# Block products in the third chunk's feed-forward layer, with block weights and raw weights in buffers of their own

## The chip, the cores and the metric

One core of a Trainium2 chip runs the whole program. TensorE (PE) multiplies, VectorE (DVE) and ScalarE (ACT) work on elements, GpSimd (POOL) mostly issues DMAs here, and SyncE (SP) issues DMAs alone. The metric is the device time of one execution in microseconds (us). A profiled execution adds a span (first to last instruction) and the busy times of the engines.

## The reference

Two layers, each an attention block and a feed-forward block with residual additions, on x of 2048 rows and 576 columns, float32:

```python
def _A_ref(x, wqkv, wo):            # 32 heads of 18, window of 8 keys, dilation 2
    q, k, v = split(x @ wqkv)
    kg, vg = k[:, :, idx], v[:, :, idx]          # idx = pos - 2 * (0..7), masked below 0
    attn = softmax(einsum("bhsd,bhswd->bhsw", q, kg) * 18 ** -0.5)
    return einsum("bhsw,bhswd->bhsd", attn, vg) @ wo
def _B_ref(x, w1, w2):              # w1 576 x 4608, w2 4608 x 576
    return silu(x @ w1) @ w2
x = x + _A_ref(_layernorm(x), wqkv, wo)
x = x + _B_ref(_layernorm(x), w1, w2)
x = x + _A_ref(_layernorm(x), wqkv, wo)          # second layer, same weights
x = x + _B_ref(_layernorm(x), w1, w2)
```

## The kernel before

The rows are cut into four chunks of 512, and each chunk goes through both layers, so there are eight steps s = 0 to 7 (steps 0 to 3 are the first layer). A step is attention, the projection with wo (line 828), layer norm, and the feed-forward block. Keys, queries and values of chunks 1 to 3 in the first layer are computed during step 0 (`qkv_ahead`) and read back from HBM later.

All matrix products run in float16 halves: a value is split into a high half and a low half, and high by high, high by low and low by high are summed. The weights come as float32. ACT makes the high halves with a scale that is worked out from the squares of the weights, DVE makes the low halves, and the halves are stored to HBM (`w1s`, `w2s`, `wqs`) for the later steps. For w1 and w2 this happens in step 0, in `raw_load` and `raw_split`.

There are two forms of the feed-forward block. Steps 0 to 2 use `ffn`: for each of 36 slices of 128 hidden columns, 14 matmuls of 512 columns (line 1167), silu, splitting, and then the second product (line 1186, 72 matmuls of 288 columns for three slices and one block of rows). Steps 3 to 7 use `ffn_pairs`: two slices are taken together, and the first product of the pair is put together from seven block products of sums and differences (line 1071, seven matmuls of 256 columns each, 49 for a pair), in the manner of Strassen. `forms` makes the seven sums of the normalized input for a chunk, and DVE and ACT add up the products (lines 1075 and 1078) before silu. The second product is the same in size (line 1125). The 18 pairs go in groups of 5, 4, 5 and 4 (`G2`); 7 block weights and 2 slices of w2 are loaded for each.

The block weights are made once, by `prepare`, for each of the 18 pairs: POOL issues 12 DMAs that load a pair's w1 (lines 966 and 969), DVE makes three more sums (977), ACT makes the high halves (985), DVE the low halves (992), and POOL stores the seven block weights as `wfs` (997). They are loaded again by SP (`w<-wfs`).

What order the work has is settled at build time by a planner (`Plan.order`): each operation has an engine, an assumed duration and a priority (lower goes first), and the planner hands out buffers and writes each engine's instructions in one order. On the chip each engine follows its order and waits where data or a buffer is missing. `S2 = 3` is the first step that uses pairs, and `PREP = 1.6` is the priority of the prepares: behind the attention of step 2 (1.0) and ahead of that of step 3 (2.0). Areas of memory are shared by several kinds of buffers: `xa` (a normalized input, the prepares' output `wg`, half of the forms `yb`), `wq` (weights of q, k and v; the prepares' input `wr`, `ws`; two of the three buffers `hq` in which a pair's products are added), `w1` (six slices of w1 or twelve block weights), `w2`, `hs`, `xb`, `yo`, `o`.

At the very start `raw_wq` loads wqkv in four units of columns; each unit's five tiles are squared on ACT (line 565) before its scale is known, and then split (582 on ACT, 585 on DVE).

## Time and profile before

| What | Value |
|---|---|
| median of 3 runs | 2184.23 us (2181.3 to 2188.39) |
| profiled execution | 2180.11 us, span 2178.3 us |
| PE busy | 2125.9 us (98%) |
| DVE busy | 1585.8 us (73%) |
| ACT busy | 932.0 us (43%) |
| granted TensorE clock | 0.998 |
| HBM read, written | 298.47 MB, 67.68 MB |

The steps' feed-forward blocks follow each other on PE: in the trace that of step 0 begins at 226.9 us, of step 1 at about 473.6, of step 2 at 698.95, of step 3 (the first with pairs) at 932.2, and of step 7 at 1971.8. The attention of the next step is worked on by DVE while PE does a feed-forward block, and its matmuls stand in between. A busy share of an engine is an average over such stretches. The time the engine idles ahead of an instruction is listed with what ended that wait.

### The profile page before, as it was taken

What the parts mean: (1) busy time and instruction counts of PE and PEld (TensorE: products, weight loads), DVE (VectorE), ACT (ScalarE), POOL (GpSimd) and SP (SyncE); (2) the same over time, 40 slices, a digit from 0 to 9 for tenths busy, and PEclk for the clock granted to TensorE, in tenths of its full rate; (3) what the DMA queues carried; (4) which work ended last, traced back from release to release, by engine and by line L of the source; (5) the groups of instructions that cost most, each with busy time, mean ns of one, the idle gap of its engine ahead of it and who ended that gap; (6) DMA issues with size and microseconds to landing.
All of it is one profiled execution on the core that took longest, in us unless ns stands there. A gap on an engine that the chain in (4) does not pass through costs nothing.

```text
span 2178.3 us, 40221 instructions
## 1 busy us (share of the span) xinstructions
PE 2125.9 (98%) x15820; PEld 1540.8 (71%) x15820; DVE 1585.8 (73%) x2479; ACT 932.0 (43%) x1715; POOL 379.4 (17%) x639
## 2 busy tenths in 40 slices
PE   5999999999999999999999999999999999999999
PEld 3555556656766666677788778887688867888887
DVE  7898999999999754457975599646995569852222
ACT  7545677744244334343324434243442424333232
POOL 2124365332234331301100010000000000000000
PEclk9999999999999999999999999999999999999999
DMA  5577577586677675786649675496655855575443
GB/s 160 161 199 271 177 237 237 182 297 218 170 256 255 171 214 167 209 261 192 191 108 246 169 209 174 112 260 158 202 170 141 240 160 149 161 185 174 142 149 108
DMA packets 314006, 416.07 MB, mean 191 GB/s; under 512 B 136904, under 2 KB 237876, under 8 KB 307544
## 3 DMA queue, kind: packets, MB, share of 16 engines
q1 hardware_dynamic: 274832, 279.13, 45.2%
q0 software_dynamic: 35712, 129.17, 18.3%
q10 hardware_dynamic: 3272, 5.19, 0.8%
q8 instruction: 124, 2.03, 0.4%
q14 instruction: 66, 0.54, 0.1%
HBM read 298.47 MB, written 67.68 MB: 168 GB/s over the span
## 4 chain that ended last, share of the span: by engine, by line
PE 71%; DVE 15%; DMA 7%; issue 3%; POOL 1%; ACT 1%; ACTq 0%; SPq 0%; DVEq 0%; POOLq 0%
PE acc L1125 23%; PE z L1071 10%; PE misc L1071 10%; PE acc L1186 7%; PE z L1167 6%; PE z L658 6%; PE misc L658 5%; PE acc L828 4%; DVE pr L789 2%; DVE lg L760 2%; DMA w<-wfs 2%; DVE pr L796 2%; DVE pr L756 2%; DMA wq<-in_B_w_dram 1%; DVE xa L992 1%
## 5 line engine op out<-in xcount | busy, mean ns | idle before, releaser
L1125 PE MATMUL acc<-w,h 128*128 128x288 f16 x4320 | 544.9, 286 | 1.5 <-DVE h L1104 0.7
L1125 PEld LDWEIGHTS <-h 128*128 128x128 f16 x4320 | 422.5, 98 | 108.6 <-DVE h L1104 1.0
L1071 PEld LDWEIGHTS <-w 128*128 128x128 f16 x4410 | 430.8, 98 | 64.4 <-DMA w<-wfs 7.4
L1167 PE MATMUL z<-xb,w 128*128 128x512 f16 x1512 | 331.8, 379 | 6.4 <-ACT w L902 2.0
L1186 PE MATMUL acc<-w,h 128*128 128x288 f16 x2592 | 321.9, 286 | 0.0
L1186 PEld LDWEIGHTS <-h 128*128 128x128 f16 x2592 | 253.7, 98 | 65.7
L1071 PE MATMUL z<-xb,w 128*128 128x256 f16 x2240 | 281.9, 273 | 2.5 <-DMA w<-wfs 1.3
L1071 PE MATMUL misc<-xb,w 128*128 128x256 f16 x2170 | 273.4, 273 | 5.5 <-DMA w<-wfs 4.5
L1167 PEld LDWEIGHTS <-w 128*128 128x128 f16 x1512 | 147.5, 98 | 182.3 <-DVE w L904 3.7
L835 DVE SCALAR_TENSOR_TENSOR x<-acc,d,x 128x576 f32<-128x576 f32 x135 | 109.5, 812 | 192.3 <-PE acc L1125 151.5
L658 PEld LDWEIGHTS <-xa 128*128 128x128 f16 x1344 | 132.3, 99 | 119.6 <-issue 10.1
L756 DVE TENSOR_TENSOR pr<-qt,kv 128x2304 f32<-128x2304 f32 x64 | 163.5, 2554 | 33.6 <-DMA kv<-kv 32.2
L789 DVE TENSOR_TENSOR pr<-kv,pe 128x1152 f32<-128x1152 f32 x128 | 169.7, 1352 | 1.1
L760 DVE TENSOR_REDUCE lg<-pr 128x128 f32<-128x2304 f32 x64 | 163.1, 2548 | 1.2
L796 DVE TENSOR_TENSOR pr<-pr 128x1152 f32<-128x1152 f32 (+1 forms) x128 | 135.2, 1056 | 3.4
L1169 ACT ACTIVATE hs<-z,d 128x512 f32<-128x512 f32 x108 | 73.8, 683 | 123.1 <-PE z L1167 121.4
L1104 DVE SCALAR_TENSOR_TENSOR h<-wq,sh,h 128x1024 f16<-128x1024 f32 x59 | 75.5, 1280 | 60.9 <-ACT h L1101 60.9
L658 PE MATMUL z<-wq,xa 128*128 128x432 f16 x602 | 116.3, 349 | 3.4 <-ACT w L671 3.1
L828 PE MATMUL acc<-wo,yo 128*128 128x288 f16 x896 | 115.7, 288 | 3.3 <-DMA yo<-yh 3.3
L658 PE MATMUL misc<-wq,xa 128*128 128x432 f16 x574 | 111.8, 351 | 4.0 <-ACT xa L448 2.5
L1174 DVE SCALAR_TENSOR_TENSOR h<-hs,sh,h 128x512 f16<-128x512 f32 x108 | 79.6, 746 | 45.6 <-ACT h L1171 45.5
L1075 ACT ACTIVATE wq<-misc 128x256 f32<-128x256 f32 x85 | 32.0, 376 | 187.0 <-PE misc L1071 187.0
(196 smaller groups left out, 2355.1 us busy)
## 6 DMA issues: line engine op xcount, KB each, us to landing
w<-wfs SPq DMA_DIRECT2D x630, 160.0 KB, 3.3
w<-w2s SPq DMA_DIRECT2D x252, 288.0 KB, 4.8
w<-w1s SPq DMA_DIRECT2D x72, 320.0 KB, 4.8
wfs<-xa POOLq DMA_DIRECT2D x18, 1120.0 KB, 5.7
wq<-wqs SPq DMA_DIRECT2D x17, 1080.0 KB, 7.0
kv<-kd POOLq DMA_DIRECT2D x8, 1584.0 KB, 8.2
w1s<-w POOLq DMA_DIRECT2D x36, 320.0 KB, 3.8
w<-in_B_w_dram POOLq DMA_DIRECT2D x36, 288.0 KB, 4.6
```

Source lines behind the costliest of these rows:

```text
L658: nc.tensor.matmul(T(m)[:, :3 * UC], a, b, start=n == 0, stop=n == len(pl) - 1)
L756: nc.vector.tensor_tensor(T(pr), T(qt)[:, j:j + 2, None, :].to_broadcast([P, 2, W, UC]), win(T(kv), j, 2), op=ALU.mult)
L760: nc.vector.tensor_reduce(T(lg)[:, j:j + 2].rearrange("p a w h -> p (a w h)"), T(pr).rearrange("p a w (h d) -> p (a w h) d", d=DH), axis=A ...
L789: nc.vector.tensor_tensor(T(pr)[:, a].rearrange("p w (h d) -> p w h d", d=DH), v, T(pe)[:, j + a, :, :, None].to_broadcast([P, W, UH, DH]) ...
L796: nc.vector.tensor_tensor(t[:, :, 0:h, :], t[:, :, 0:h, :], t[:, :, h:2 * h, :], op=ALU.add)
L828: nc.tensor.matmul(T(acc)[:, h, 0:288], a, b[:, h * 288:(h + 1) * 288], start=n == 0, stop=n == len(pl) - 1)
L835: nc.vector.scalar_tensor_tensor(t, T(acc)[:, :, 0:288], d, t, op0=ALU.mult, op1=ALU.add)
L1071: nc.tensor.matmul(t, w[:, u, :], v[:, r, :], start=first and m == 0, stop=m == 6, skip_group_check=True)
L1125: nc.tensor.matmul(T(acc)[:, h, 0:288], T(hb[t])[:, a, f, j * P:(j + 1) * P], T(wbs[t][f])[:, w, h * 288:(h + 1) * 288], start=t == 0 and ...
L1167: nc.tensor.matmul(T(z), v, u, start=m == 0, stop=m == len(pl) - 1)
L1174: op("DVE", 0.68, lambda hs=hs, h=h, f=f: nc.vector.scalar_tensor_tensor(T(h)[:, 1, :], T(hs), shs[i][:, f:f + 1], T(h)[:, 0, :], op0=ALU. ...
L1186: nc.tensor.matmul(T(acc)[:, h, 0:288], T(hb[q])[:, a, j * P:(j + 1) * P], T(wbs[q][0])[:, w, h * 288:(h + 1) * 288], start=q == 0 and m = ...
```

## The change

Step 2 uses pairs as well (`S2 = 2`), so the prepares must be done for it. They get the priority 0.9, ahead of the attention of step 2. So that they can overlap with step 2's feed-forward block, buffers are placed anew. The block weights are stored in two parts from two buffers, `wg` with four rows and `wh` with three, and a pair's load waits only for its part. The forms of step 2 use `yc`, which lies in the second of the two key and value buffers, in place of `yb`. The products of a pair are added in `ha` (in the areas `hs`, `xb` and `yo`) up to step 6. The prepare's load is made of 8 DMAs instead of 12, for the same bytes; the last 32 rows of each half are read four times through a step of zero.

In step 0, from slice 6 on (`FAR = 6`), raw w2 goes to `wu` (in `xa`) and the halves of w1 to `wv` (in `wq`), where before both shared the buffers of `w1` and `w2`. And at the start, the squares of the second unit of wqkv wait until ACT has made the fourth high half of the first unit. Some assumed sizes for the planner are changed too, and fetches and sums of attention 3 wait for step 2's forms.

```diff
+FAR = 6
-PREP = 1.6
-S2 = 3
+PREP = 0.9
+S2 = 2
...
-    part("wg", XA, 1, [7, 5, P], F16)
+    part("wg", XA, 1, [4, 5, P], F16)
+    part("wh", XA, 1, [3, 5, P], F16, at=4 * KB * 2)
...
-    tag("kv", 2, [P, NI, 2, UC], F32)
+    KVB = NI * 2 * UC * 4
+    KV = area("kvs", 2 * KVB, F32)
+    part("kv", KV, 2, [NI, 2, UC], F32)
+    part("yc", KV, 1, [8, KH], F32, at=KVB, turns=False)
...
+    part("wv", WQA, 6, [10, P], F16)
+    part("wu", XA, 4, [2, D], F16)
...
+    parts("ha", [(HSA, 0), (XB, 14 * KB * 2), (YO, 0)], [4, 2 * P], F32)
...
-            op("ACT", 0.7 + (1.3 if u == 0 and k == 0 else 0), square, [rs[k]], [("accq", u, k)], WQ[u])
+            op("ACT", 0.7 + (1.3 if u == 0 and k == 0 else 0), square, [rs[k]], [("accq", u, k)], WQ[u], after=highs[3:4] if u else ())
...
-            op("ACT", 0.57, hi, [rs[k], ("su", u)], [w.keys[k]], WQ[u])
+            highs.append(op("ACT", 0.57, hi, [rs[k], ("su", u)], [w.keys[k]], WQ[u]))
...
-        a, b = raws[f] = Buf("w1"), Buf("w2")
+        far = f >= FAR
+        a, b = raws[f] = Buf("w1"), Buf("wu" if far else "w2")
...
-        wab = [(Buf("w1"), Buf("w2")) for f in fs]
+        far = f0 >= FAR
+        wab = [(Buf("wv" if far else "w1"), Buf("w2")) for f in fs]
...
-            for i in range(4):
-                f, h = divmod(i, 2)
-                c = slice((2 * q + f) * P, (2 * q + f + 1) * P)
-                nc.gpsimd.dma_start(t[:, i, 0:2, :], w1[h * KH:h * KH + 2 * P, c].rearrange("(k p) c -> p k c", p=P))
-            for r in range(4):
-                for h in range(2):
-                    nc.gpsimd.dma_start(t[32 * r:32 * (r + 1), h:4:2, 2, :], w1[
-                        h * KH + 2 * P:(h + 1) * KH, 2 * q * P:(2 * q + 2) * P].rearrange("p (f c) -> p f c", f=2))
-        op("POOL", 7.2, load, ["wsc"], [w], prio, nbytes=P * 12 * P * 4, lanes=8)
+            for h in range(2):
+                for k in range(2):
+                    nc.gpsimd.dma_start(t[:, h:4:2, k, :], w1[h * KH + k * P:h * KH + (k + 1) * P, 2 * q * P:(2 * q + 2) * P].rearrange(
+                        "p (f c) -> p f c", f=2))
+                for f in range(2):
+                    v = w1[h * KH + 2 * P:(h + 1) * KH, (2 * q + f) * P:(2 * q + f + 1) * P]
+                    nc.gpsimd.dma_start(t[:, h + 2 * f, 2, :], bass.AP(tensor=v.tensor, offset=v.offset, ap=[[0, 4], *v.ap]))
+        op("POOL", 4.8, load, ["wsc"], [w], prio, nbytes=P * 12 * P * 4, lanes=8)
...
-        op("POOL", 0.57, lambda: nc.gpsimd.dma_start(wfs[q], T(g).rearrange("p i a b -> p (i a b)")), [(g, 0), (g, 4)],
-           [("wfs", q)], prio, nbytes=P * 7 * KB * 2)
+            op("POOL", 0.57, lambda g=g, r0=r0, r1=r1: nc.gpsimd.dma_start(
+                wfs[q][:, r0 * KB:r1 * KB], T(g).rearrange("p i a b -> p (i a b)")), [(g, 0)], [("wfs", q, r0 // 4)], prio, nbytes=P * n * KB * 2)
...
-                hq, h = Buf("hq"), Buf("hp")
+                hq, h = Buf("hq" if s >= NC - 1 else "ha"), Buf("hp")
...
-        XT[s] = layer_norm(X[s], s - 1.0, "xb", s == 1, s == 0) if s < S2 else forms(X[s], s - 1.0)
+        XT[s] = layer_norm(X[s], s - 1.0, "xb", s == 1, s == 0) if s < S2 else forms(X[s], s - 1.0, "yc" if s == S2 else "yb", [("wfs", NP - 1, 1)] if s == S2 + 1 else [])
```

In the changed kernel the lines lie some 9 to 16 further down: 565 becomes 577, 582 becomes 594, 977 becomes 992, 992 becomes 1007, 997 becomes 1012, 1078 becomes 1094 and 1104 becomes 1120.

The first place is ACT at the start: `junk` with 128x432 are the squares of wqkv, `yo` and `yh` the first rows normalized, `wq` the high halves, `xa` the transposed input. Before:

```order
L565 ACT_TABLE_LOAD
L565 ACTIVATE junk,accq<-h 128x432 x9
L522 ACTIVATE yo<-x_74,nt_99 128x576
L525 ACTIVATE yh<-yo,nt_99 128x576
L582 ACTIVATE wq<-h,su 128x432 x4
L448 ACTIVATE xa<-acc_105 128x9x128
```

And in the changed kernel:

```order
L577 ACT_TABLE_LOAD
L577 ACTIVATE junk,accq<-h 128x432 x5
L534 ACTIVATE yo<-x_74,nt_98 128x576
L537 ACTIVATE yh<-yo,nt_98 128x576
L594 ACTIVATE wq<-h,su 128x432 x4
L457 ACTIVATE xa<-acc_104 128x9x128
L594 ACTIVATE wq<-h,su 128x432
```

Four squares of the second unit, which stood ahead of the first normalization, have moved behind the high halves.

The second place is POOL with the prepares, between the second and third steps' feed-forward blocks. `wq` is here the area that takes the raw weights. Before:

```order
L997 DMA wfs_207<-xa 128x4480
L966 DMA wq<-in_B_w_dram 128x2x128 x4
L969 DMA wq<-in_B_w_dram 32x2x128 x8
L997 DMA wfs_208<-xa 128x4480
L966 DMA wq<-in_B_w_dram 128x2x128 x4
```

And in the changed kernel:

```order
L1012 DMA wfs_209<-xa 128x2560
L1012 DMA wfs_209<-xa 128x1920
L713 DMA kvs<-kd_241 128x3168
L715 DMA qt_84<-qd_233 128x576
L1012 DMA wfs_210<-xa 128x2560
L1012 DMA wfs_210<-xa 128x1920
L981 DMA wq<-in_B_w_dram 128x2x128 x2
L985 DMA wq<-in_B_w_dram 128x1x128 x2
```

A store has become two, and a load of 12 issues one of 8 (two such pairs of rows).

The third place is DVE where step 2's feed-forward block begins. `pr`, `lg` and `pe` belong to attention 3, `x` to the second product, `h` to the low halves of the hidden values, `wq<-wq` and `xa` to a prepare. Before:

```order
L1174 SCALAR_TENSOR_TENSOR h<-hs,sh_267,h 128x512
L774 TENSOR_REDUCE mx_91<-pe_88 128x32
L775 RECIPROCAL mx_91<-mx_91 128x32
L776 TENSOR_TENSOR pe_88<-pe_88,mx_91 128x256
L789 TENSOR_TENSOR pr_89<-kv_83,pe_88 128x1152
L1174 SCALAR_TENSOR_TENSOR h<-hs,sh_267,h 128x512
L977 TENSOR_TENSOR wq<-wq 128x384 x4
```

And in the changed kernel:

```order
L1007 SCALAR_TENSOR_TENSOR xa<-wq,accw,xa 128x3x128
L848 SCALAR_TENSOR_TENSOR x_81<-acc_104,d_269,x_81 128x576
L1094 TENSOR_TENSOR hs<-z_100,hs 128x256
L1094 TENSOR_TENSOR hs<-misc_102,hs 128x256
L1094 TENSOR_TENSOR hs<-z_101,hs 128x256
L769 TENSOR_TENSOR pr_88<-qt_84,kvs 128x2304
L1094 TENSOR_TENSOR yo<-misc_102,yo 128x256
L1094 TENSOR_TENSOR yo<-misc_103,yo 128x256
L1120 SCALAR_TENSOR_TENSOR h<-hs,sh_267,h 128x1024
```

In the order of before, DVE reaches this place with the sums of prepare 9 of 18, in the last of attention 3's four units. In the changed order 13 of the 18 prepares stand ahead of the first addition for a pair, and the other five in between the pairs; attention 3 is here at its second unit.

## The prediction

> **What bounds the kernel.** I read the page first: the busy times, and then the chain that ended last by engine.

> ```profile
> span 2178.3 us, 40221 instructions
> PE 2125.9 (98%) x15820; PEld 1540.8 (71%) x15820; DVE 1585.8 (73%) x2479; ACT 932.0 (43%) x1715; POOL 379.4 (17%) x639
> PE 71%; DVE 15%; DMA 7%; issue 3%; POOL 1%; ACT 1%; ACTq 0%; SPq 0%; DVEq 0%; POOLq 0%
> ```

> PE idles 2178.3 - 2125.9 = 52.4 us in all. A busy PE may still be slow, so I cut the span at the steps' feed-forward blocks and read the busy times by stretch. Behind the comma stand the busy us of PE, PEld (weight loads), DVE, ACT and POOL, then the granted clock, the DMA share and GB/s; the two rows of the second fence are of PE alone.

> ```profile
> 226.90:473.60 246.70, 240.88 (x1590) 154.00 (x1590) 234.24 (x364) 167.36 (x287) 117.06 (x204) 1.00 0.68 225
> 473.60:698.95 225.35, 225.35 (x1469) 143.44 (x1467) 221.66 (x274) 88.29 (x117) 70.68 (x119) 1.00 0.71 226
> 698.95:932.20 233.25, 229.92 (x1482) 145.33 (x1480) 134.80 (x235) 88.17 (x139) 73.93 (x124) 0.99 0.69 199
> 932.20:1190.00 257.80, 256.30 (x2075) 202.38 (x2074) 188.61 (x293) 100.79 (x202) 20.70 (x33) 1.00 0.68 193
> 1190.00:1450.00 260.00, 256.65 (x2077) 202.92 (x2076) 186.44 (x291) 95.78 (x196) 16.40 (x28) 1.00 0.67 181
> 1450.00:1711.00 261.00, 257.80 (x2086) 203.62 (x2084) 184.96 (x286) 96.12 (x196) 10.65 (x20) 1.00 0.66 181
> 1711.00:1971.80 260.80, 259.26 (x2101) 205.24 (x2100) 182.61 (x280) 95.78 (x196) 10.66 (x20) 1.00 0.63 177
> 1971.80:2178.30 206.50, 202.28 (x1746) 170.59 (x1744) 57.12 (x90) 67.13 (x126) 0.54 (x1) 1.00 0.45 141
> ```

> ```profile
> 0.00:49.20 49.20, 25.65 (x165) 1.00 0.61 172
> 49.20:226.90 177.70, 171.75 (x1047) 0.99 0.64 198
> ```

> The reader sees three things. PE is the bound from 226.9 us to the end: it idles 5.8 us in step 0's block, 0 in step 1's, 3.3 in step 2's, and 1.5, 3.4, 3.2, 1.5 and 4.2 in the five blocks with pairs. Nearly half of all its idling, 23.6 us, lies in the first 49.2 us. And DVE is nearly as full in steps 0 and 1 (221.66 of 225.35 us in the second row), but has 98.5 us free in step 2's block, the one that is changed. So a change pays by the work that it takes off PE, and by idle time at the start, as long as DVE and the loads keep up.

> **Term 1, the first product of step 2.** What a matmul takes in a stream is read from long pieces of the chain, which are start, length and what:

> ```profile
> 771.43 27.20 PE z L1167 x126
> 798.62 26.46 PE acc L1186 x216
> 932.39 3.06 PE z L1071 x28
> 2000.01 27.93 PE acc L1125 x228
> ```

> A matmul of 512 columns takes 27.20 / 126 = 0.2159 us, one of 256 takes 3.06 / 28 = 0.1093. The second product costs 0.1225 us a matmul in both forms (26.46 / 216 and 27.93 / 228), and has 864 of them in either. Direct: 36 x 14 x 0.2159 = 108.8 us. Pairs: 18 x 49 x 0.1093 = 96.4 us. This takes 12.4 us off PE, and in step 2's block (third row) PE works 229.92 of 233.25 us, so it is all on the path: -12.4.

> [...]

> **Term 2, the squares at the start.** Here are, in this order, rows of ACT, of DVE and of PE from the timeline. In brackets stands the idle time ahead and what ended it.

> ```profile
> 12.80 0.19 ACT L565 ACTIVATION_READ_ACCUMULATOR junk<-h 128x1 f32 x1
> 15.79 0.56 ACT L565 ACTIVATE junk<-h 128x432 f16<-128x432 f32 x1 [2.80 <-DMA h<-in_A_wqkv_dram]
> 18.88 0.76 ACT L522 ACTIVATE yo<-x,nt 128x576 f32<-128x576 f32 x1
> 20.36 2.28 ACT L582 ACTIVATE wq<-h,su 128x432 f16<-128x432 f32 x4
> ```

> ```profile
> 13.97 0.16 DVE L476 TENSOR_SCALAR nt<-mv 128x4 f32<-128x4 f32 x1
> ```

> ```profile
> 20.50 0.61 PE L446 MATMUL acc<-ident,yh 128*128 128x128 f16 x4 [3.06 <-ACT yh L525]
> 24.71 5.22 PE L658 MATMUL misc<-wq,xa 128*128 128x432 f16 x14 [2.51 <-ACT xa L448]
> ```

> The first unit's squares end at 13.0, and the normalization's numbers `nt` are there at 14.1. Yet ACT next has four squares of the second unit in its order, whose load lands at 15.8, and so the normalization begins at 18.88. With the squares behind, it can begin at 14.15: 4.7 us earlier. PE's first real product follows later on. From the rows' lengths: the row block on ACT ends at 15.7, the four high halves at 18.0, and DVE needs until about 20.9 for the low halves of two row blocks and of the weights, which it makes one after the other. PE's transposes then end at 21.4, so the product at 24.71 moves to about 21.5. That is -3.2 us. The bounds are -4.7 (all of it) and 0 (the second unit's weights come too late by as much, since its own squares now come later). Of the stretch behind, 49.2 to 226.9, PE works 171.75 of 177.70 us, so an earlier start is passed on.

> **Term 3, waits of step 2's block.** Its 3.3 us of idle is a single row:

> ```profile
> 740.77 4.93 PE L828 MATMUL acc<-wo,yo 128*128 128x288 f16 x28 [3.33 <-DMA yo<-yh]
> ```

> The first row below is DVE's, the second is one of the chain.

> ```profile
> 727.84 0.51 DVE L815 TENSOR_SCALAR yh<-o,so 128x576 f16<-128x576 f32 x1
> 729.90 10.82 DMA yo<-yh
> ```

> The projection of chunk 3 (line 828) stands on PE at 740.77, and its first input was made by DVE only at 727.84. In the changed order PE meets it later, behind 686 matmuls of the pairs' first product and 552 of the second: 698.95 - 3.2 + 686 x 0.1093 + 552 x 0.1225 = 838 us. On DVE, the order's rows up to this input, each priced with the mean of its group, come to 91 us more than before: 727.84 + 91 - 3.2 = 816 us, if DVE never waits. So 22 us are left for the rest of the input's split and for the transposing DMA, which took 10.8 us there. The old wait of 3.3 may go wholly, or come again: I take half, -1.7, bounds -3.3 and +3.3.

> Pairs bring waits of their own. The five blocks with pairs idle 1.5 to 4.2 us, 2.8 on average, the one cause that stands out being late block weights:

> ```profile
> PE misc L1071 <- DMA w<-wfs: 4.5, 3, 2.4
> ```

> I take +2.8 for the new block of pairs; bounds +1.5 and +12 (second rival).

> **What is costed at nothing.** DVE gets 4 additions and a split of 1024 columns for a pair, and loses two splits of 512:

> ```profile
> L1174 DVE SCALAR_TENSOR_TENSOR h<-hs,sh,h 128x512 f16<-128x512 f32 x108 | 79.6, 746 | 45.6 <-ACT h L1171 45.5
> L1104 DVE SCALAR_TENSOR_TENSOR h<-wq,sh,h 128x1024 f16<-128x1024 f32 x59 | 75.5, 1280 | 60.9 <-ACT h L1101 60.9
> L1078 DVE TENSOR_TENSOR wq<-z,wq 128x256 f32<-128x256 f32 x92 | 37.7, 419 | 21.5 <-ACT wq L1075 12.8 <-PE z L1071 8.6
> ```

> That is 18 x (4 x 0.419 + 1.280 - 2 x 0.746) = 26.4 us. Steps 1 and 2 together have 221.66 + 134.80 = 356.5 us of DVE work in 458.6 us; with 26.4 more in 12.4 less it is 383 of 446, still covered. If the cover goes, PE waits in its second products, as rival 1 says. The prepares are only moved. Their 12 DMA issues become 8 and their one store becomes two, 10 for 13 on POOL, which works 70.68 and 73.93 us in the two stretches: no cost. Where the waits `after` are added (fetch and sums of attention 3 behind the forms), what queues behind them on POOL are prepares' loads; with 13 of 18 prepares ahead of the pairs I cost that at nothing too. Step 0's new buffers can change its 5.8 us of idle either way; PE has no other slack there, so I take 0, bounds -5.8 and +5.8.

> **The sum.** -12.4 - 3.2 - 1.7 + 2.8 = -14.5 us. The profiled execution took 2180.11 us (span 2178.3), 4.1 below the median of 2184.23. So it becomes 2165.6, and the median 2169.7. With all bounds at their best it is -12.4 - 4.7 - 3.3 + 1.5 - 5.8 = -24.7, or 2159.5.

> **Rival 1, slower: the prepares come too late.** A pair's products wait for its `wfs`. The stores in the profile before:

> ```profile
> L997 POOL DMA_DIRECT2D wfs<-xa x18: 537/569/804, 535.9 to 945.1; - x18
>   DVE xa L992: 101.9, 11
> DMA to landing us min/median/max: 5.1/5.7/8.6
> w<-wfs SPq DMA_DIRECT2D x630, 160.0 KB, 3.3
> ```

> 18 stores from 535.9 to 945.1 are one in 24.1 us. In the new order 43 us less DVE work stand ahead of the first sums (436 for 479 us, priced as above), so the first store comes at about 535.9 - 43 = 493. At the old pace the last is issued at 493 + 17 x 24.1 = 903, and is loaded 5.7 + 3.3 us later, at 912. PE needs it at 695.8 + 17 x 5.36 (first products) + 14 x 48 x 0.1225 (second products of three groups) + 112 x 0.1225 (a projection) = 883. It would wait 29 us, and the sum turns to +14: 2199 us. This decides once the pace is above 22.4 us a prepare. Against it speaks that the store's waits are for DVE (101.9 us of them), that is, for an order which put attention first; the new order puts 13 prepares ahead of the first pair. Chance 0.12.

> **Rival 2, no change: loads starve the pairs.** A pair's loads are 7 x 160 + 2 x 288 KB against 2 x (320 + 288) KB, 8.6 MB more for 18, which over 220 us is 39 GB/s on top of the 226 that step 1's block with prepares shows at a share of 0.71. If each of the four groups then waits some 3 us for a load (the longest such wait in the trace is 2.4), the waits are +12 in place of +2.8: -5.3, or 2178.9 us, within the bound of no change. Chance 0.10; at this bandwidth no row shows PE waiting, but none shows pairs.

> **Rival 3, no change: the narrow products gain nothing.** By busy time, not by the stream, the products of both forms cost a pair the same:

> ```profile
> L1167 PE MATMUL z<-xb,w 128*128 128x512 f16 x1512 | 331.8, 379 | 6.4 <-ACT w L902 2.0
> L1071 PE MATMUL z<-xb,w 128*128 128x256 f16 x2240 | 281.9, 273 | 2.5 <-DMA w<-wfs 1.3
> ```

> 331.8 / 1512 x 28 = 6.14 us and 281.9 / 2240 x 49 = 6.17 us. Then term 1 is 18 x 0.03 = +0.5, and the sum -1.6: 2182.6 us. But busy intervals of neighbours in different banks overlap and are counted in both lines, so the chain's 3.06 us for 28 is the better measure. Chance 0.03. [...]

> **Rival 4, no change: the start is not passed on.** The second unit's weights come later by what the first gains, and step 0's new order waits 5.8 us more: -14.5 + 3.2 + 5.8 = -5.5, 2178.7 us. DVE, which follows the same chain at the start, speaks against. Chance 0.07.

> **The numbers.** The forecast, 2169.7 us, has a chance of 0.68. A measurement of this kernel tells a change of about 0.3% (6.5 us, so below 2177.7 is faster and above 2190.8 slower). Faster is the forecast, 0.68; same are rivals 2, 3 and 4, 0.20; slower is rival 1, 0.12. The range goes from 2158, the sum of the best bounds with a little for the runs' spread, to 2185, which takes in rivals 2 to 4 and leaves out rival 1. The forecast's own range is 2160 to 2177.

> **What would show it.** Term 1: step 2's block has 882 matmuls of 256 columns, and PE's busy time falls by about 12 us. Term 2: ACT's first `yo` begins near 14 us and the first product of 14 near 21.5. Term 3: the row of PE's waits for `yo<-yh` shrinks, and that for `w<-wfs` stays below 9 us. Rival 1 would show as PE waiting for `w<-wfs` at the end of the third step, rival 2 as waits spread over all four groups. The prediction fails if PE idles more than 50 us in all, or if DVE, full until chunk 3's projection, comes to it later than PE does.

## The result: no change

The changed kernel takes 2185.23 us (median of 14 runs, 2177.21 to 2187.70), the kernel before 2184.54 us in the same session (14 runs, 2179.49 to 2190.68). The ratio is 1.000 with a 95% interval of 0.999 to 1.001. The forecast was 2169.7 us, so 15 us of expected gain are missing. The profiled execution took 2186.47 us with a span of 2184.3 us, against 2180.11 and 2178.3 before.

One thing in the words ahead of the prediction is wrong: the products of a pair are added in `ha` in step 2 alone, and not up to step 6. The line reads `Buf("hq" if s >= NC - 1 else "ha")` with four chunks, so steps 3 to 7 use `hq` as they did before. No term of the prediction rests on it.

### The profile page after: what moved, and what is told of

It is laid out like the page before. It is cut to its first block, busy times and chain, and to the rows that moved or that the text cites. A ratio compares the mean times of both kernels' runs of the same rounds, so it can differ in the third digit from the quotient of the medians.

```text
span 2184.3 us, 41276 instructions
## 1 busy us (share of the span) xinstructions
PE 2119.9 (97%) x16198; PEld 1578.8 (72%) x16198; DVE 1605.7 (74%) x2539; ACT 954.5 (44%) x1795; POOL 364.3 (17%) x585
## 4 chain that ended last, share of the span: by engine, by line
PE 81%; DVE 8%; DMA 7%; ACT 2%; issue 1%; POOL 1%; SPq 0%; ACTq 0%; DVEq 0%
PE acc L1141 25%; PE misc L1087 11%; PE z L1087 11%; PE z L670 8%; PE acc L1202 8%; PE z L1183 7%; PE misc L670 5%; PE acc L841 4%; DMA w<-wfs 3%; DVE lg L773 1%; DVE pr L802 1%; DVE pr L769 1%; DVE pr L809 1%; DMA w<-w2s 1%; DMA wq<-in_B_w_dram 1%
## 5 line engine op out<-in xcount | busy, mean ns | idle before, releaser
L1087 PEld LDWEIGHTS <-w 128*128 128x128 f16 x5292 | 518.9, 98 | 97.3 <-DMA w<-wfs 21.4
L1087 PE MATMUL z<-xb,w 128*128 128x256 f16 x2653 | 339.2, 275 | 14.0 <-DMA w<-wfs 9.9
L1087 PE MATMUL misc<-xb,w 128*128 128x256 f16 x2639 | 333.9, 273 | 10.4 <-DMA w<-wfs 8.6
L769 DVE TENSOR_TENSOR pr<-qt,kvs 128x2304 f32<-128x2304 f32 x64 | 163.4, 2553 | 34.6 <-DMA kvs<-kvs 24.7
L802 DVE TENSOR_TENSOR pr<-kvs,pe 128x1152 f32<-128x1152 f32 x128 | 169.9, 1352 | 1.1
L1183 PE MATMUL z<-xb,w 128*128 128x512 f16 x588 | 130.8, 383 | 6.0 <-ACT w L918 2.4
L841 PEld LDWEIGHTS <-yo 128*128 128x128 f16 x896 | 88.1, 99 | 27.1 <-DMA yo<-yh 2.7
L750 POOL DMA_DIRECT2D kvs<-kvs x64 | 33.8, 535 | 374.8 <-ACT qt L740 348.1
L1183 PE MATMUL z<-xb,wq 128*128 128x512 f16 x420 | 93.2, 379 | 0.7 <-ACT hs L1185 0.7
```

The lines of the kernel that those rows point to most:

```text
L769: nc.vector.tensor_tensor(T(pr), T(qt)[:, j:j + 2, None, :].to_broadcast([P, 2, W, UC]), win(T(kv), j, 2), op=ALU.mult)
L802: nc.vector.tensor_tensor(T(pr)[:, a].rearrange("p w (h d) -> p w h d", d=DH), v, T(pe)[:, j + a, :, :, None].to_broadcast([P, W, UH, DH]) ...
L841: nc.tensor.matmul(T(acc)[:, h, 0:288], a, b[:, h * 288:(h + 1) * 288], start=n == 0, stop=n == len(pl) - 1)
L1087: nc.tensor.matmul(t, w[:, u, :], v[:, r, :], start=first and m == 0, stop=m == 6, skip_group_check=True)
L1183: nc.tensor.matmul(T(z), v, u, start=m == 0, stop=m == len(pl) - 1)
```

## The profile after

The page's first lines and its chain by engine:

```profile
span 2184.3 us, 41276 instructions
PE 2119.9 (97%) x16198; PEld 1578.8 (72%) x16198; DVE 1605.7 (74%) x2539; ACT 954.5 (44%) x1795; POOL 364.3 (17%) x585
PE 81%; DVE 8%; DMA 7%; ACT 2%; issue 1%; POOL 1%; SPq 0%; ACTq 0%; DVEq 0%
```

PE's busy time fell by 6.0 us and its idle time rose from 52.4 to 64.4 us. Where that lies is read from the same cuts as before: the start, step 0's attention, the feed-forward blocks of steps 0, 1 and 2, and all the rest. The last fence has the rest of the kernel before. Columns as in the prediction: busy us of PE, PEld, DVE, ACT, POOL, then granted clock, DMA share and GB/s.

```profile
0.00:43.00 43.00, 23.99 (x165) 14.69 (x166) 33.70 (x122) 31.61 (x65) 11.55 (x24) 1.00 0.69 192
43.00:220.76 177.76, 171.50 (x1046) 98.28 (x1045) 162.08 (x250) 98.57 (x188) 47.27 (x67) 0.99 0.63 196
220.76:467.15 246.39, 241.14 (x1592) 154.51 (x1590) 231.65 (x366) 170.83 (x292) 121.99 (x210) 0.99 0.71 231
467.15:698.39 231.24, 227.51 (x1468) 143.72 (x1466) 205.32 (x297) 104.14 (x158) 83.78 (x124) 0.99 0.84 244
698.39:932.14 233.75, 219.66 (x1861) 182.39 (x1858) 175.32 (x269) 98.14 (x183) 41.22 (x60) 0.98 0.79 227
932.14:2184.30 1252.16, 1236.14 (x10076) 985.18 (x10073) 797.65 (x1239) 451.20 (x910) 58.49 (x101) 1.00 0.61 173
```

```profile
932.20:2178.30 1246.10, 1232.30 (x10076) 984.74 (x10074) 799.74 (x1240) 455.61 (x916) 58.95 (x102) 1.00 0.63 176
```

| Stretch | before | after | difference |
|---|---|---|---|
| until step 0's block begins | 226.9 | 220.76 | -6.1 |
| step 0's block | 246.7 | 246.4 | -0.3 |
| step 1's block | 225.35 | 231.24 | +5.9 |
| step 2's block (the one with new pairs) | 233.25 | 233.75 | +0.5 |
| steps 3 to 7 | 1246.1 | 1252.16 | +6.1 |

So the start gave its gain and step 1 gave it back. In step 2's block PE works 219.66 us for 229.92, as hoped, but it idles 14.1 us for 3.3. PE's rows there, from the timeline:

```profile
709.85 2.62 PE L1141 MATMUL acc<-w,h 128*128 128x288 f16 x20 [1.64 <-DVE h L1120]
720.89 1.68 PE L1087 MATMUL z<-xb,w 128*128 128x256 f16 x7 [8.42 <-DMA w<-wfs]
731.59 0.93 PE L1087 MATMUL z<-xb,w 128*128 128x256 f16 x7
732.36 0.93 PE L1087 MATMUL misc<-xb,w 128*128 128x256 f16 x7
```

One wait, 8.42 us for a block weight of the second pair, is 60% of the idle time. Behind it seven matmuls took 1.68 us, where a row of seven takes 0.93 further on: the granted clock was 0.53 from 720.90 to 727.00 us. What SP's queue did in that place (rows of the queue's own timeline, then of its waits between 680 and 760 us):

```profile
692.71 9.82 SPq L858 DMA_DIRECT2D w<-w2s x9
705.01 31.62 SPq L1017 DMA_DIRECT2D w<-wfs x24
```

```profile
SPq L1017 <- DMA w<-w2s: 12.6, 7, 2.8
SPq L858 <- PE acc L1202: 5.3, 8, 3.0
```

Nine loads of w2 (288 KB each) stand ahead of the second pair's last block weights. They wait for buffers that step 1's last products free, and the block weights behind them then wait 12.6 us more for w2 loads to land. The reason is in the trace: in this program SP's loads take turns on eight semaphores, and each waits until the eighth one ahead of it has landed. The block weight's load at 705.01 us waits so for the w2 load that was issued at 693.44. At 688 us, 5 us ahead of the w2 loads, POOL had issued two fetches of attention 3; the DMA view of 670 to 735 us has them as

```profile
kvs<-kd POOLq DMA_DIRECT2D x2, 1584.0 KB, 10.6
```

so either the order on SP's queue or the burst of bytes could be the cause. That was the first question for experiments. The second was why the start's gain did not arrive.

## The experiments

All were timed against the kernel before on the same chip; a ratio within 0.003 of 1 is no change by the prediction's bound.

**Block weights ahead of w2.** In the first group of step 2, the w2 loads of the first three pairs go behind these pairs' block weights (`wfl[2]` is the last load of those):

```diff
-                w2b = [load_w2(2 * q + f, pd) for f in range(2)]
+                if g or s > S2:
+                    w2b = [load_w2(2 * q + f, pd) for f in range(2)]
+                else:
+                    if q == 2:
+                        first = [load_w2(f, pd, after=[wfl[2]]) for f in range(6)]
...
```

> The changed kernel, but in the first group of step 2 the loads of w2 for the first three pairs stand on SP's queue behind the block weights of those pairs. Queue theory: the wait of 8.42 us for w<-wfs at 720.89 came from the nine w2 loads (2.6 MB) ahead of the block weights. It falls below 2 us, the halved clock of 10.24 us behind it goes as well, and the time falls by 8.4 + 5.1 = 13 us, to about 2172 (ratio 0.994). Rival, burst theory: the transfers were slow since the fetches of attention 3 (3.75 MB), two stores and a prepare's loads fell into the same 10 us; the block weights then still land late, a wait of 4 us or more stays in the first three pairs, and the time falls by less than 5 us.

It took 2173.35 us, ratio 0.9956 (0.9941 to 0.9971): faster than both kernels. Step 2's block (its row among the stretches) and SP's queue at its start:

```profile
698.65:920.58 221.93, 218.50 (x1868) 181.88 (x1865) 173.65 (x272) 98.27 (x184) 41.20 (x60) 1.00 0.82 241
```

```profile
699.60 10.89 SPq L1019 DMA_DIRECT2D w<-wfs x14
714.31 7.19 SPq L858 DMA_DIRECT2D w<-w2s x8
```

PE idles 3.4 us there in place of 14.1, the granted clock is 1.00 where it was 0.98, and the block is 11.8 us shorter. That is the whole difference of the medians (11.9, or 11.0 when each is set against its own runs of the kernel before). So with these bytes the queue's order decides. The expectation had counted 5.1 us for the halved clock; of that stretch of 10.24 us 4.55 lay inside the wait itself, and PE worked 5.17 us of it, so it cost some 2.6 us by estimate.

The order alone does not make the wait, though. In the kernel before, step 3's block, which begins at 932.23 us and also follows the direct form, has the same nine loads ahead of block weights:

```profile
926.54 7.31 SPq L845 DMA_DIRECT2D w<-w2s x9
933.95 7.70 SPq L1002 DMA_DIRECT2D w<-wfs x10
```

PE does not wait for block weights in the first 17 us of that block. What differs most is the traffic in the ten us ahead of the block (the first row is the kernel before, the second the changed kernel; the DMA share is the last number but one):

```profile
922.00:932.00 10.00, 10.00 (x84) 7.98 (x83) 6.70 (x12) 0.83 (x2) 1.08 (x2) 1.00 0.58 180
688.00:698.00 10.00, 10.00 (x84) 8.00 (x82) 7.05 (x9) 3.20 (x4) 3.57 (x7) 1.00 1.01 384
```

In weights_first the share is 1.04 from 698.65 to 712.40 us, with no such wait. So in these three kernels the long wait took both, this order and DMA engines at a share of 1.01.

**The burst of fetches taken away.** The four fetches of attention 3 are planned behind the products of pairs 0, 2, 4 and 8 of step 2:

```diff
+FETCH = (0, 2, 4, 8)
-                   after=formed[-1:] if u else ())
+                   after=prods[7 * FETCH[u] + 6:7 * FETCH[u] + 7] if prods else formed[-1:] if u else ())
```

> The changed kernel, but the four fetches of attention 3 (kvs and qt, 1.87 MB each) wait in the planner for the first products of pairs 0, 2, 4 and 8 of step 2, so that the first two no longer stand at 688 us, 10 us ahead of the block. The nine w2 loads stay ahead of the block weights. Burst theory: the wait of 8.42 us falls below 3 us, with the halved clock behind it, and the time falls by 8 to 12 us, to 2173 to 2177. Queue theory: the w2 loads still hold up the block weights, the wait stays above 5 us, and the time falls by less than 4 us. DVE gets the first fetch some 12 us later, which it has room for.

It took 2204.92 us, ratio 1.0105 (1.0083 to 1.0128). PE's rows, and two stretches of step 2's block:

```profile
718.72 4.10 PE L1090 MATMUL z<-xb,w 128*128 128x256 f16 x21 [4.83 <-DMA w<-wfs]
941.70 1.67 PE L1090 MATMUL misc<-xb,w 128*128 128x256 f16 x7 [12.22 <-DMA xb<-yo]
```

```profile
738.00:778.00 40.00, 37.44 (x319) 30.95 (x318) 38.63 (x46) 13.91 (x22) 8.13 (x13) 1.00 0.78 237
778.00:818.00 40.00, 37.84 (x326) 31.89 (x326) 38.56 (x45) 23.21 (x38) 13.70 (x20) 1.00 0.87 272
```

The wait fell from 8.42 to 4.83 us, so the fetches have a share in it; the w2 loads, the stores and a prepare's loads stayed. And "which it has room for" was wrong: DVE is busy 38.6 of 40 us in the middle of the block, attention 3 comes late, and with it step 3's forms, for which PE waits 12.22 us at 941.70.

**The start alone.** The kernel before, with only the squares moved:

```diff
-            op("ACT", 0.7 + (1.3 if u == 0 and k == 0 else 0), square, [rs[k]], [("accq", u, k)], WQ[u])
+            op("ACT", 0.7 + (1.3 if u == 0 and k == 0 else 0), square, [rs[k]], [("accq", u, k)], WQ[u], after=highs[3:4] if u else ())
```

> The kernel before, with one part of the change: the squares of the second unit stand behind the first unit's fourth high half. In the changed kernel step 0's block begins 6.3 us earlier than before (220.76 for 227.03). Theory: that is this part alone, and everything behind it moves with it, so the median falls by some 6 us, to about 2178.5 (ratio 0.997). Rival: the gain at the start is taken back by step 0's own waits, or the 6.3 us came from the new buffers of step 0: then the block begins less than 2 us earlier and the ratio is 1.000.

It took 2186.06 us, ratio 1.0009 (0.9998 to 1.0020): nothing, though the first product of 14 came at 18.54 us (24.71 before) and step 0's block begins at 220.67. The largest loss is in step 1:

```profile
18.54 5.22 PE L659 MATMUL misc<-wq,xa 128*128 128x432 f16 x14 [1.52 <-ACT xa L448]
573.74 5.27 PE L829 MATMUL acc<-wo,yo 128*128 128x288 f16 x28 [4.71 <-DMA yo<-yh]
```

```profile
SPq L450 <- PE z L1168: 9.4, 1, 9.4
```

The last of the four transposing DMAs of chunk 2's projection stood 9.4 us on SP's queue waiting for PE: there are two buffers for the transposed inputs (`oT`), and an earlier row block's product had still to read one. The row of 28 matmuls takes 5.27 us, where one in the kernel before takes 3.59 (551.46 us): halved clock again, with a granted clock of 0.98 over the 110 us from 470 to 580. Together 4.7 + 1.7 = 6.4 us. That is not the whole account; the rest is shown with the next kernel.

**The start alone, with that place spaced out.** As above, with three times the assumed size for those four DMAs, so that the planner puts other products between the row blocks:

```diff
-                  nbytes=P * 9 * P * 4)
+                  nbytes=P * 9 * P * 4 * slow)
...
+            transposed(oh, lambda oT=oT: T(oT), oT, j, pr_, s < 2, 3 if s == 2 else 1)
```

> The kernel start_only (the kernel before with the squares moved), but the planner assumes three times the size for the transposing DMAs of chunk 2's projection, so that PE's order has other products between its four row blocks. In start_only PE waited 4.71 us for yo<-yh at 573.74, with half clock behind it (1.7 us): the fourth transpose stood for 9.4 us on SP until a buffer came free that the second row block's product reads. Theory: the early start was lost in this one place of the order; the wait falls below 1 us and the median to 2178 to 2180 (ratio 0.998). Rival: the vector work bounds steps 0 and 1, so that the wait comes back elsewhere in step 1 or 2 and the ratio stays at 1.000 to 1.001.

It took 2177.36 us, ratio 0.9970 (0.9954 to 0.9985). No wait for `yo<-yh` above 0.7 us is left, and the time is what the theory said. The way to it is another. Below are PE's rows from the start of step 0's block to that of step 2's, and from there to that of step 3's, for the kernel before, for start_only and for start_spaced:

```profile
227.03:698.95 471.92, 466.23 (x3057) 1.00 0.69 225
698.95:932.23 233.28, 229.95 (x1483) 0.99 0.69 199
```

```profile
220.67:702.98 482.31, 468.58 (x3058) 1.00 0.70 224
702.98:931.32 228.34, 228.34 (x1483) 1.00 0.67 201
```

```profile
220.80:700.09 479.29, 468.65 (x3058) 1.00 0.69 225
700.09:929.01 228.92, 228.50 (x1482) 1.00 0.69 201
```

PE does the same matmuls in all three. On the way to step 2's block start_only loses 10.4 us against the kernel before and start_spaced still 7.4, of which 5.0 are idle time, most of it in step 0's block. So the early start does not reach step 2's block in either. What both gain lies in step 2's block, 4.9 and 4.4 us shorter than before: the old wait of 3.3 us for `yo<-yh` and its halved clock have gone. The spacing brought back 2.9 us of step 1's loss (700.09 for 702.98). What it is worth without the early start was not tried.

**The changed kernel without new pairs in step 2.** Step 3's forms keep their place `yb`, and nothing waits in the order for step 2's forms, which there are none of:

```diff
-S2 = 2
+S2 = 3
...
-        formed.append(done)
```

> The changed kernel with pairs from step 3 on, as before (and so without the order of step 3's attention behind the forms of step 2); the start, step 0's buffers, the 8 loads and the early prepares stay. Theory: step 2's pairs as they run now are worth little (their 12.4 us of PE time against 14 us of waits and 5 us of halved clock in that block, less the 3.3 us that it waited before), so this kernel is about as fast as the changed one, 2181 to 2187, and its step 1 block still shows the wait of some 2 us for yo<-yh with a stretch of halved clock behind it. Rival: the pairs gain their 12.4 us, and what takes it back is elsewhere (the early prepares): then this kernel is slower than before, 2192 or more.

It took 2193.01 us, ratio 1.0045 (1.0029 to 1.0062). The rival was right: it is slower than the changed kernel, so within this change the pairs gain, and the rest costs. PE's rows say where:

```profile
612.32 5.08 PE L841 MATMUL acc<-wo,yo 128*128 128x288 f16 x28 [6.95 <-DMA yo<-yh]
782.26 5.28 PE L841 MATMUL acc<-wo,yo 128*128 128x288 f16 x28 [3.49 <-DMA yo<-yh]
793.00 5.19 PE L841 MATMUL acc<-wo,yo 128*128 128x288 f16 x28 [2.44 <-DMA yo<-yh]
```

The inputs of the projections of chunks 2 and 3 are late, by 12.9 us in all. The likely reason is the prepares, which are now planned ahead of attention. The changed kernel has 2.2 us of such waits; its order is another one, with chunk 3's projection behind a block of pairs.

**The prepares later.** The kernel weights_first with `PREP = 1.05` in place of 0.9:

> The kernel weights_first with the prepares' priority at 1.05 instead of 0.9, so behind the attention of chunk 2 and ahead of that of chunk 3. This is the first rival of the prediction, made on purpose. If the early place of the prepares costs step 1 its waits (yo<-yh 0.95 + 2.57 us and 1.7 us of halved clock), and a pace of some 10 us a prepare suffices behind it, the median falls by up to 5 us, to 2168 to 2171. If the block weights then come too late, PE waits for w<-wfs at the end of step 2's third group, some 5 to 30 us in all: 2178 to 2205. I think the second likelier, since in the changed kernel the last store is issued only at 829.9 us and PE reads the last pair at about 880.

It took 2195.50 us, ratio 1.0049 (1.0031 to 1.0068). The second case came, but at another place than I had named:

```profile
709.39 1.70 PE L1095 MATMUL z<-xb,w 128*128 128x256 f16 x14 [2.85 <-DMA w<-wfs]
937.27 1.68 PE L1095 MATMUL z<-xb,w 128*128 128x256 f16 x7 [8.57 <-DMA xb<-yo]
```

Step 1 has no wait for `yo<-yh` above 0.7 us any more, which bears out what the early prepares cost there. But block weights are late in the first group, and what costs most is again step 3's forms. Between 740 and 860 us, in the middle of step 2's block, DVE now works 38.1 us for the prepares (lines 992 and 1007), for 23.0 in weights_first, and comes to attention 3 too late. So in this order the later place of the prepares costs more than it saves.

**Step 0's new buffers undone.** The kernel weights_first with

```diff
-FAR = 6
+FAR = 36
```

> The kernel weights_first without step 0's new buffers: raw w2 and the halves of w1 share w1 and w2 in all of step 0, as before the change. Both profiles wait about as much in step 0's block (5.8 us before, 5.25 in the changed kernel), so the theory is that this part is worth nothing: 2171 to 2176. Rival: the buffers carry some of the change's gain, since step 1's block can start only when step 0's last loads have landed: 2178 or more.

It took 2200.13 us, ratio 1.0072 (1.0054 to 1.0090), 27 us more than weights_first. PE waits in step 0's block, and ACT for raw weights (waits from 226 to 470 us of this kernel, and of weights_first):

```profile
281.19 7.89 PE L1191 MATMUL z<-xb,w 128*128 128x512 f16 x28 [4.25 <-ACT hs L1193]
ACT junk L899 <- DMA w<-in_B_w_dram: 19.1, 7, 4.6
```

```profile
ACT junk L899 <- DMA w<-in_B_w_dram: 3.2, 4, 1.7
```

The kernel before has 20.6 us of such waits of ACT and yet little idle of PE, so what the buffers are worth depends on the order around them. Why this order needs them was not tried.

**The start undone.** The kernel weights_first without the squares' move:

```diff
-            op("ACT", 0.7 + (1.3 if u == 0 and k == 0 else 0), square, [rs[k]], [("accq", u, k)], WQ[u], after=highs[3:4] if u else ())
+            op("ACT", 0.7 + (1.3 if u == 0 and k == 0 else 0), square, [rs[k]], [("accq", u, k)], WQ[u])
```

> The kernel weights_first with one part of the change undone: the second unit's squares stand ahead of the high halves again. PE's order is the same in both as far as the end of step 1. Theory, by the first four runs: the start is not passed on, since in step 1 PE comes to the projection of chunk 2 earlier than its transposed inputs (yo<-yh), and what it is early there it waits; weights_first waited 0.95 + 2.57 us there, with 3.4 us of halved clock behind (1.7 us), 5.2 in all. Without the early start these go, and the median is 2174 to 2176. Rival: the early start is worth its 6.3 us: 2179 or more.

It took 2175.28 us, ratio 0.9964 (0.9949 to 0.9978). The time is as the theory said, the mechanism is not: its waits for `yo<-yh` are 0.72 and 2.60 us, as with the early start.

```profile
607.91 8.71 PE L841 MATMUL acc<-wo,yo 128*128 128x288 f16 x56 [2.60 <-DMA yo<-yh]
```

That row stands 4.0 us behind the same one of weights_first (603.95), and the profiled ends 1.7 us apart. So in these two profiles some of the start is passed on; whether any of it shows in the medians, the intervals leave open.

**Spacing and queue order together.** Three kernels put the projection's spacing into weights_first, with the w2 loads of three, two or four pairs behind the block weights:

> The kernel weights_first with the same spacing of chunk 2's projection. weights_first waits 0.95 + 2.57 us there and has 3.4 us of halved clock behind it. Theory: both go, and the start's gain reaches the end: 5 us less, 2168 to 2170 (ratio 0.993 to 0.994). Rival: as before, the vector work is late there, and the wait only moves: 2172 to 2174.

> The kernel wf_spaced, but only the w2 loads of the first two pairs stand behind the block weights, and those of the third pair's ahead. wf_spaced lost its gain to a wait of 3.02 us for w<-w2s at 712.75 (w2 now too late, PE's order begins the second products in the third pair) and 1.7 us of halved clock behind it. Theory, the queue's order sets which of the two loads is late: with the w2 loads one pair earlier the wait for w2 falls below 1.5 us and none above 2 us for w<-wfs comes in its place: 2169 to 2172. Rival: what is late is the sum of the bytes, and the wait comes back as one for w<-wfs of 3 us or more: 2174 to 2178.

> The kernel wf_spaced, but the w2 loads of the first four pairs stand behind the block weights of those pairs. wf_spaced began step 2's block 8.3 us earlier than weights_first (690.31 for 698.65) and lost it there to waits of 1.26 us for w<-wfs and 3.02 us for w<-w2s, with 1.7 us of halved clock; wf1_spaced, with w2 further ahead, waited 4.85 us for w<-wfs. Here PE's order has 203 matmuls of first products ahead of the first second product, where it had 140 and 119. Theory: both loads are in time, since w2 is wanted last, no wait above 1.5 us stands in the first 40 us of the block, and the median is 2167 to 2170. Rival: when PE comes earlier, the transfers of that stretch (share of the DMA engines 0.9 to 1.1) are late in whatever order they stand; a wait of 3 us or more comes again, 2173 to 2178.

They took 2175.60 us (ratio 0.9967, 0.9953 to 0.9980), 2177.97 us (0.9970, 0.9954 to 0.9986) and 2175.12 us (0.9966, 0.9955 to 0.9978). None beats weights_first. The first one's rows, and one of each of the others:

```profile
690.31 3.22 PE L1095 MATMUL z<-xb,w 128*128 128x256 f16 x28
712.75 3.04 PE L1149 MATMUL acc<-w,h 128*128 128x288 f16 x12 [3.02 <-DMA w<-w2s]
```

```profile
717.66 1.67 PE L1095 MATMUL misc<-xb,w 128*128 128x256 f16 x7 [4.85 <-DMA w<-wfs]
```

```profile
716.58 0.94 PE L1095 MATMUL z<-xb,w 128*128 128x256 f16 x7 [1.29 <-DMA w<-wfs]
```

The spacing did its work: in the first one step 2's block begins at 690.31, 8.6 us ahead of the kernel before (694.13 and 694.75 in the others), and no wait for `yo<-yh` above 0.7 us is left. But in the first two PE then meets the loads earlier than they can land, and the lateness comes back as a wait for w2 or for block weights. The third has only small waits there, 1.29 us for a load and 1.00, 0.58 and 0.56 us for sums of ACT and DVE. It bears out the half of its theory that no large wait remains, and misses the time; where the rest of its lead goes was not followed up.

**Another queue for wq.** The kernel weights_first with the wq loads of steps 4 to 7 issued by POOL:

> The kernel weights_first, but the loads of wq in steps 4 to 7 (1.1 MB each) are issued by POOL instead of SP. In all kernels with pairs PE waits 0.8 to 2.5 us for w<-wfs some 90 to 110 us into the blocks of steps 3 to 7; on SP's queue a wq load stands there that waits 7.5 us for PE's reading of the old wq, ahead of block weights. Theory: queued behind it the block weights come late; on POOL's queue the wq load holds nothing up, these waits (some 7 us in all, with one or two stretches of halved clock) fall by half or more, and the median falls by 4 to 6 us, to 2167 to 2170. Rival: the 1.1 MB transfer itself slows the block weights: no change, 2172 to 2175.

It took 2185.89 us, ratio 1.0001 (0.9984 to 1.0017): 12 us slower than weights_first, so this theory falls. Waits for block weights grew (weights_first has 6.4 us in the first row's place), and on SP's queue w2 loads now stand at the head for longer (waits between 1180 and 1450 us; the third fence is weights_first):

```profile
PE z L1096 <- DMA w<-wfs: 11.5, 4, 3.8
```

```profile
SPq L859 <- PE acc L1150: 63.2, 29, 36.1
```

```profile
SPq L858 <- PE acc L1149: 34.4, 28, 15.1
```

It looks as if the planner, with wq out of the queue, puts w2 ahead of block weights for longer; this was not tried.

## Why the prediction was wrong

**Term 1 was right.** PE works 219.66 us for 229.92 in step 2's block. Of this the halved clock takes some 2.6 us after and 1.4 before, which leaves 217.1 for 228.5: -11.4, where -12.4 was forecast. (weights_first, with no halved clock in that block, has 218.50, which would make it -10.0.) The third rival is out: rows of seven matmuls begin 0.77 us apart (731.59 and 732.36), 0.110 us each. That is the duration the sum had taken (0.1093). Each of these rows lasts 0.93 us and so runs 0.16 us into the next; in the profile before PE's groups by line sum to 2244.0 us of busy time for 2125.9, which is why busy time by line was the wrong price.

**Term 2 held at the start, and failed in "so an earlier start is passed on".** ACT's first `yo` begins at 13.96 us (forecast: near 14), the first product at 20.64 (forecast: 21.5), and step 0's block 6.1 us earlier, which is more than the best bound of 4.7. The reason given, that PE works 171.75 of 177.70 us of the stretch behind, says only that nothing is lost in that stretch. The changed kernel keeps the gain through step 0's block and loses 5.9 us in step 1's, where PE comes to the projection of chunk 2 ahead of its inputs. The early start alone does not explain that wait: wf_no_start has it without the early start, and wf_prep_later, with the early start and later prepares, has none. In the kernel before, start_only shows that the gain can be lost at the same projection (6.4 us) and in other waits of steps 0 and 1 (some 4 us). This is the fourth rival, by another wait than the one it named.

**Term 3 failed in "I take +2.8 for the new block of pairs".** The old wait of 3.3 us for `yo<-yh` in step 2 did go: chunk 3's projection has none. But the times worked out for it were off on both sides. DVE made its first input at 846.06 us, where "816 us, if DVE never waits" was forecast, and PE came to it at 858.74 (forecast: 838), held back by the block's waits and halved clock. In weights_first the two are at 829.98 and 848.20, so there too the order keeps them apart. But the waits of pairs came to 14.1 us, above the upper bound of +12. The 2.8 were a mean over five blocks. One of them, step 3's, also follows the direct form and has the same w2 loads at the queue's head, but it idles 1.5 us: the DMA engines had a share of 0.58 ahead of it. Ahead of the new block it is 1.01, with prepares' loads, stores and fetches under way, and the w2 loads that wait for the old form's last products hold up the block weights. The second rival named the starving loads, but as "each of the four groups then waits some 3 us for a load"; it was a single place, and the order counted as much as the bytes, since weights_first removes it with the same bytes.

**Where the difference lies.** The forecast was -14.5 us, and this profile's span is 6.0 us longer. Of the 20.5 us between them step 2's block has 11.8 (+0.5 for -12.4 - 1.7 + 2.8), the start and the blocks of steps 0 and 1 have 2.7, and steps 3 to 7 have 6.1. The median is 15.5 us above the forecast.

**What was missing: the halved clock behind some waits.** No term had it. PE works 22.22 us at a granted clock of 0.50 after, and 6.14 us before; by estimate half of that is lost, some 11 us after and 3 us before (below).

**What was "costed at nothing".** The move of the prepares was not free: in pairs_from_3 it shows as 12.9 us of waits at the two projections, and step 1's block in the changed kernel is 5.9 us longer (3.7 us idle, 1.7 us of halved clock). That DVE is "still covered" held in the changed kernel, but barely: the two experiments that move vector work to later make PE wait 8.6 and 12.2 us for step 3's forms. The mean of 134.80 of 233.25 us before could not show it: in the changed kernel DVE is full for a third of the block, 78.1 of the 80 us from 740 to 820. And step 0's buffers, "I take 0, bounds -5.8 and +5.8", were worth 27 us in the one order where they were undone.

The first rival did not come about in the changed kernel. Brought about on purpose (wf_prep_later), it gave 2195.5 us where 2199 were worked out, but by late forms rather than by late block weights of the third group, so that the numbers are near each other is luck.

Steps 3 to 7, whose blocks of pairs the change leaves as they were, are 6.1 us longer in this profile: 2.2 us more idle time, and two stretches of halved clock (at 1685.73 and 1815.44 us, 1.7 us each) where the profile before has none. The runs of the changed kernel spread from 2177.21 us at a mean granted clock of 0.998 to 2187.70 at 0.994, so part of this is chance.

## What to carry to other kernels

When a stage changes its form, read the queues at its beginning, not the mean of other stages: what stands ahead of the first new load, what does it wait for, and how full are the DMA engines? The same nine loads at the head cost nothing at a share of 0.58 and 8.42 us at 1.01. A gain ahead of a meeting point (a projection whose input comes through a DMA with two buffers) is passed on only if the other side is early too; look for the next such point and its slack before a gain is summed. And where a planner writes the order, a change of a few microseconds in one place moves PE to places where other waits are, so each part needs a run of its own. And look at the granted clock behind a wait: in these traces 52 of the 69 waits of PE of 2 us or more had halved clock behind them, and so cost more than their length.

## What the runs showed of the hardware

The clock behind a wait was not expected. Three stretches of the changed kernel around its long wait (712.47 to 720.89):

```profile
712.40:720.90 8.50, 0.08 (x2) 0.01 (x1) 2.45 (x1) 0.00 (x0) 4.97 (x7) 0.73 1.07 278
720.90:727.00 6.10, 5.59 (x28) 3.90 (x29) 4.33 (x5) 2.40 (x4) 0.00 (x0) 0.53 1.04 282
727.00:737.25 10.25, 10.25 (x94) 8.88 (x92) 8.43 (x13) 7.18 (x12) 0.00 (x0) 1.00 0.55 157
```

The granted clock is 0.50 from 716.34 to 726.58 us, and 1.00 again behind it. Behind the first 45 us, and without the very end, the profile before has two stretches at half clock and that of the changed kernel six. Seven of the eight last 3.41 us, the one above 10.24. (In the profile before they begin at 166.66 and 740.10 us, in that of the changed kernel at 159.97, 238.48, 590.05, 716.34, 1685.73 and 1815.44.)

The length of a wait alone does not tell: in the changed kernel a wait of 2.08 us (to 1685.09) has a stretch behind it, and one of 2.52 us (to 1031.66) has none.
